# Batched causal attention feeding a maxout MLP: three TensorE score regions per group made two, with a tile of scores in the shared PSUM pool and early tokens copied first

## The chip, the cores and the metric

One core of a Trainium2 chip runs the whole kernel. The time is device microseconds of one launch; eight runs of the kernel before were taken. Tokens, heads and weights are all handled by that core, so the engines in question are its own: TensorE (PE), VectorE (DVE), ScalarE (ACT), GpSimd (POOL) and the queue that issues transfers (SP).

## The reference

Block-causal attention over 8 batches, 8 heads, 576 positions and head size 64, and behind it, on the same tokens, a maxout MLP:

```python
B, H, S, D = q.shape                      # 8, 8, 576, 64
scores = scale * np.matmul(q, k.transpose(0, 1, 3, 2))
mask = (pos[:, None] // 64) >= (pos[None, :] // 64)     # causal by blocks of 64
attn = exp(scores - max) / sum            # softmax over the allowed keys
x = (attn @ v).transpose(0, 2, 1, 3).reshape(B * S, H * D)   # 4608 tokens x 512
out = np.maximum(x @ w1, x @ w2) @ w_out  # 512 -> 1024 -> 512, float32
```

## The kernel before, in words

**Work units.** Heads are taken in pairs (`p`, 32 in all: 4 a batch), pairs in groups of two (`g`, 16 in all: 2 a batch). The two heads of a pair lie on partitions 0 to 63 and 64 to 127 and are multiplied as two 64-row tiles of the PE array side by side; everything with a contraction of 128 (the MLP, and attention times v) uses the whole array. A pair goes through: load and cast of q and k (`load_qk`, `cast`), 18 transposes of 64x64 for q and 18 for k of a whole group (`transposes`, L303) with a copy out of PSUM by DVE and ACT (`copy_out`, L310), scores (`scores`, L321, and `corner_scores`, L339), exp by ACT into `aT` (`exp`, L345, L401), zeroing of masked corners by POOL (`mask`, L350), attention times v in two groups of matmuls of 65 columns (`av`, L429: query tiles 0 and 1 with 6 matmuls, 2 to 4 with 24), a division by DVE (L435, L436), and transposes of the result into `xT` (`x_out`, L451, L453), which DVE copies out (L456, L457). `xT` is what the MLP reads.

**The MLP** is cut into spans of tokens (256, 320, then 512 each). For a span, `h_unit` makes eight times two accumulations of four matmuls (L197), one for w1 and one for w2: DVE copies the first out of PSUM (L204) and takes the maximum with the second (L206). `y_unit` makes eight matmuls with w_out (L215), copied out by ACT (by DVE for the first two spans, L221), and sent off. `units` lists all of these in order, `steps` matmul by matmul, and `fill(n)` emits the next `n` of them (in units of a 512-column matmul) if their tokens are done. So MLP matmuls are placed by hand between attention work, and all engines execute the order as it is written (`manual_schedule`).

**PSUM** has two pools: `ps_s`, two buffers of two banks each, for scores; `ps_m`, four buffers of one bank, for everything else: transposes, attention times v, x_out, h, y.

**Stages.** A prologue written out by hand covers batch 0 (groups 0 and 1): the scores of the first 256 queries first (`burst_p`), then those of the rest (`burst_q1` to `burst_q3`), so that the first 256 tokens reach the MLP early; `warm_up(n)` puts in matmuls of zeros whose result nobody reads. Then the loop over g from 2 to 15. In it each group has three stretches in which the array is in two 64-row tiles, called regions here: x_out of the group before with score tiles 0 and 1 of pair a; transposes of q with tile 2 of a and tile 0 of b; transposes of k with tiles 1 and 2 of b. In the second and third the exps come before the copies of the transposes:

```python
        for p, tiles in ((a, lambda: (tile_2(a), tile_0(b))), (b, lambda: (tile_1(b), tile_2(b)))):
            fill(hi)
            if g > GPB:
                av_with(p - LAG, lo)
            else:
                fill(lo)
            copy_out = t_pair(p)
            region(*tiles())
            copy_out()
```

Between regions `fill` emits MLP matmuls; `av_with` puts `lo = n // 18` of them between the two groups of a pair's attention times v. After the loop come the last pairs and what is left of the MLP.

Of the kernel before, what the change touches and what calls it, by code (L numbers as in the profile page):

```python
# [8 lines left out]
FP32 = mybir.dt.float32  # L9
# [5 lines left out]
def kernel(  # L15
# [95 lines left out]
    def load_qk(g, queues, gated=False):  # L111
        b, u = divmod(g, GPB)
        for nm, src, queue in (("q", q, queues[0]), ("k", k, queues[1])):
            if queue is None:
                continue
            raws[nm, g] = t = raw.tile([P, 2, RPP * D], FP32, name=f"{nm}raw")
            if gated:
                nc.gpsimd.memset(t[:, 0, :1], 0.0)
            queue.dma_start(
                out=t[:],  # L120
                in_=src[b, 4 * u:4 * u + 4].rearrange(
                    "(s h) (p t) d -> (h p) s (t d)", h=2, t=RPP),
            )

    def cast(nm, g, parts):
        t = raws.pop((nm, g)).rearrange("p s (t d) -> p t s d", d=D)
        qk_n[nm, g] = n = qkn.tile([P, RPP, 2, D], BF16, name=f"{nm}n")
        for copy, j0, j1 in parts:
            copy(out=n[:, j0:j1], in_=t[:, j0:j1])  # L129
# [12 lines left out]
    def load_w(f0, fw, which=(0, 1)):  # L142
        for i in which:
            dst, src = ((w1_sb, w1r), (w2_sb, w2r))[i]
            nc.gpsimd.dma_start(out=dst[:, :, f0:f0 + fw], in_=src[:, :, f0:f0 + fw])
# [11 lines left out]
    nc.vector.memset(zeros[:], 0.0)  # L157
    nc.scalar.activation(out=warm[:], in_=warm[:], func=AF.Exp)
    load_qk(1, (SP, SP))
    load_qk(2, (SP, None))  # L160
    make_identity(nc, ident)
    for r in range(NV):
        nc.vector.memset(vv_r[r][:, :, :, D:D + 1], 1.0)
# [9 lines left out]
    load_w(0, 256, (0,))  # L173
    cast("k", 1, ((pool, 0, RPP),))
    load_w(0, 256, (1,))
    load_qk(2, (None, SP), gated=True)


    done_tokens = [0]
# [88 lines left out]

    plan()
    steps = [(u, need, cost) for u, need, cost, n in units for _ in range(n)]  # L270
    at = [0]


# [4 lines left out]
            n += 1  # L278
        return int(total)

    def fill(n):
        while n > 0 and at[0] < len(steps) and steps[at[0]][1] <= done_tokens[0]:
            u, _, cost = steps[at[0]]
            next(u)
            n -= cost
            at[0] += 1


    def warm_up(n):
        pw = ps_m.tile([P, SPAN], FP32, name="ps_w", tag="m")  # L290
        for _ in range(n):
            nc.tensor.matmul(pw[:], zeros[:, :P], zeros[:], start=True, stop=True)
# [4 lines left out]
    def transposes(nm, g, copies):  # L297
        n = qk_n.pop((nm, g))
        pts = [ps_m.tile([P, RPP, NP], BF16, name=f"ps_{nm}T", tag="m") for _ in range(2)]
        for j in range(RPP):  # L300
            for i in range(2):
                r = slice(i * NP, (i + 1) * NP)
                nc.tensor.transpose(  # L303
                    pts[i][:, j, :], n[r, j].rearrange("p s d -> p (s d)"), ident[r, r],
                )

        def copy_out(which=(0, 1)):
            for i in which:
                t = (qT_r if nm == "q" else kT_r)[(2 * g + i) % NT]
                copies[i](  # L310
                    out=t[:, :S].rearrange("q (p j) -> q p j", j=RPP),
                    in_=pts[i].rearrange("q j p -> q p j"),
                )
        return copy_out

# [11 lines left out]
    def pad_keys(p):  # L327
        nc.gpsimd.tensor_copy(
            out=kz_r[p % NT].rearrange("p (a c) -> p a c", c=BLK)[:, 0:3:2],
            in_=kT_r[p % NT][:, S - 3 * BLK:].rearrange("p (a c) -> p a c", c=BLK)[:, 0:3:2],  # L330
        )


    def corner_scores(p, ps, col):
# [25 lines left out]
    def burst_p(p):  # L360
        burst(p, ((0, 0, QCUT), (1, P, QCUT - P)), 0)

    def burst_q1(p):
        burst(p, ((0, QCUT, 320), (1, QCUT, 192)), 384)

    def burst_q2(p):
        burst(p, ((1, 448, P), (2, QCUT, 320), (4, 512, BLK)), 896)
# [4 lines left out]
    def masks_p(p, eng=None):  # L372
        for a in (0, 256):
            mask(p, a, eng)
# [34 lines left out]
    def region(*tiles):  # L409
        for out in tiles:  # L410
            out()

    def av(p, ts):
        b, hp = divmod(p, HP)
        vv = vv_r[b % NV]
        a = aT_r[p % NA]
        n = len(ts)
        h0 = hp // 2 * 4 + hp % 2
        if p % 2 == 0 and ts[0] == 0:
            xps[p // 2] = xpool.tile([P, NCH, 2, 2, D], BF16, name="xp")  # L420
        xp = xps[p // 2]
        po = ps_m.tile([P, n, 2, D + 1], FP32, name="ps_o", tag="m")
        n_mm = 2 * sum(t + 1 for t in ts)
        mm = 0
        for gi, t in enumerate(ts):
            for hh in range(2):
                for c in range(t + 1):
                    a0 = a_col(p, c, t)
                    nc.tensor.matmul(  # L429
                        po[:, gi, hh, :], a[:, hh, a0:a0 + P], vv[:, c, h0 + 2 * hh, :],  # L430
                        start=(mm == 0), stop=(mm == n_mm - 1),
                    )
                    mm += 1
        rec = small.tile([P, 3, 2, 1], FP32, name="rec")
        nc.vector.reciprocal(rec[:, :n, :, 0], po[:, :, :, D])  # L435
        nc.vector.tensor_mul(  # L436
            xp[:, ts[0]:ts[0] + n, :, p % 2], po[:, :, :, :D],
            rec[:, :n].to_broadcast([P, n, 2, D]),
        )

    def x_out(g, t0=0, t1=NCH):
        b, u = divmod(g, GPB)
        xp = xps[g]
        n = t1 - t0
        n_odd = min(t1, NCH - 1) - t0
        pe = ps_m.tile([P, 2, n, BLK], BF16, name="ps_xe", tag="m")
        po = ps_m.tile([P, 2, n_odd, BLK], BF16, name="ps_xo", tag="m")
        for s in range(2):
            for t in range(t0, t1):
                src = xp[:, t, s].rearrange("p a d -> p (a d)")  # L450
                nc.tensor.transpose(pe[:, s, t - t0, :], src[:BLK], ident[:BLK, :BLK])  # L451
                if t < NCH - 1:
                    nc.tensor.transpose(po[:, s, t - t0, :], src[BLK:], ident[BLK:, BLK:])  # L453
        dst = xT[:, 2 * u:2 * u + 2, b * S + t0 * P:b * S + t1 * P].rearrange(
            "p s (t h w) -> p s t h w", h=2, w=BLK)
        nc.vector.tensor_copy(out=dst[:, :, :, 0], in_=pe[:])  # L456
        nc.vector.tensor_copy(out=dst[:, :, :n_odd, 1], in_=po[:])  # L457
        if u == GPB - 1:
            done_tokens[0] = min(b * S + t1 * P, (b + 1) * S)

# [37 lines left out]
        return lambda: [f() for f in outs]  # L498


    warm_up(16)
    cq = transposes("q", 0, (dve, act))
    ck = transposes("k", 0, (act, dve))
    cq((0,))
    ck((0,))
    cq((1,))
    ck((1,))
    cast("q", 1, ((dve, 0, RPP),))
    burst_p(0)
    masks_p(0)  # L510
    burst_p(1)
    warm_up(2)
    masks_p(1)
    for c in range(2, NCH):
        load_v(0, c)
    load_w(256, 256)
    cq = transposes("q", 1, (dve, dve))
    burst_q1(0)
    ck = transposes("k", 1, (dve, dve))
    for i in range(2):  # L520
        cq((i,))
        ck((i,))
    load_w(512, 512)
    warm_up(3)
    burst_p(2)
    av(0, [0, 1])
    burst_q3(0)
    warm_up(2)
    burst_p(3)
    masks_p(2, nc.vector)  # L530
    av(1, [0, 1])
    masks_p(3, nc.vector)
    burst_q2(0)
    av(2, [0, 1])
    warm_up(2)
    burst_q1(1)
    av(3, [0, 1])
    x_out(0, 0, 2)
    warm_up(2)
    cast("q", 2, ((pool, 0, RPP),))  # L540
    masks_q(0)
    cast("k", 2, ((pool, 0, RPP),))
    burst_q2(1)
    x_out(1, 0, 2)
    warm_up(2)
    burst_q3(1)
    masks_q(1)
    for c in range(3):
# [35 lines left out]
    def av_with(p, n):  # L584
        av(p, [0, 1])
        fill(n)
        av(p, [2, 3, 4])

    for g in range(GPB, NG):
        a, b = 2 * g, 2 * g + 1  # L590
        if x_due:
            x_out(x_due.pop())
        n = fill_of(g)
        region(tile_0(a), tile_1(a))
        if g == GPB:
            av(3, [2, 3, 4])
            fill(5)
            x_out(1, 2, NCH)
            n = fill_of(g)
        lo, hi = n // 18, n * 2 // 9  # L600
        for p, tiles in ((a, lambda: (tile_2(a), tile_0(b))), (b, lambda: (tile_1(b), tile_2(b)))):
            fill(hi)
            if g > GPB:
                av_with(p - LAG, lo)
            else:
                fill(lo)
            copy_out = t_pair(p)
            region(*tiles())
            copy_out()
            if p % 2 and g + 1 < NG:  # L610
                pad_keys(p + 1)
                pad_keys(p + 2)
            pool_work(p)
        if g > GPB:
            x_due.append(g - 1)
        fill(n - 2 * (lo + hi))
    for p in range(NPAIR - LAG, NPAIR):
        if x_due:
            x_out(x_due.pop())
# [40 lines left out]
```

The softmax here doesn't subtract the row's maximum and nothing guards it: scores larger than these inputs give would overflow.

## Time and profile before

| what | value |
|---|---|
| median of 8 runs (lowest, highest) | 287.0 us (286.38, 287.44) |
| the profiled execution's own time, and its span | 286.55 us, 284.7 us |
| granted TensorE clock | 1.00 |
| PE busy | 271.9 us, 96% of the span |
| DVE, ACT, POOL busy | 186.5, 140.8, 108.6 us |
| chain that ended last | PE 81%, issue 2%, ACT 2%, DVE 1% |

The span runs from the first to the last instruction of the program; 1.85 us of the execution lie around it. Busy time of PE is counted from modelled ends: a matmul of 512 columns has a row of 379 ns, while the next one starts 216 ns after it, so a busy PE isn't a PE without losses. How much is lost is read from start times.

### The profile page before, as it was taken

The numbers are of one execution on the slowest core, as the hardware profiler recorded it, in microseconds if no ns is written. First come the engines' busy times: TensorE is split into PE (matmuls) and PEld (weight loads), VectorE is DVE, ScalarE is ACT, GpSimd is POOL, SyncE is SP. The second block draws the span as 40 slices with busy tenths as digits, with TensorE's granted clock in tenths as the row PEclk, the third lists the DMA queues.
The fourth block names the chain that finished last, engine by engine and source line by source line (L and its number), as shares of the span: only waits on it lengthen the run. The fifth ranks groups of instructions, "written<-read, shape, count | busy, mean of one in ns | idle before, by whom it ended". The sixth has DMA issues, their size and how long they took to land.

```text
span 284.7 us, 7763 instructions
## 1 busy us (share of the span) xinstructions
PE 271.9 (96%) x3207; PEld 152.1 (53%) x3253; DVE 186.5 (65%) x386; ACT 140.8 (49%) x194; POOL 108.6 (38%) x271
## 2 busy tenths in 40 slices
PE   8799999899999999999999999999999999999995
PEld 2356666655555555555555464645555554444543
DVE  5867878768887576766666676667565765455430
ACT  3696567667566555573837556466454000110112
POOL 2996546764753634255243715462111000000000
PEclk9999999999999999999999999999999999999999
DMA  7999999949924893569363985176210112011114
GB/s 261 261 213 229 178 245 259 244 97 228 208 22 161 115 200 55 199 76 237 51 204 56 205 103 158 53 97 52 50 39 37 39 39 74 37 72 39 63 50 147
DMA packets 55939, 36.67 MB, mean 129 GB/s; under 512 B 38752, under 2 KB 43232, under 8 KB 55904
## 3 DMA queue, kind: packets, MB, share of 16 engines
q0 software_dynamic: 41728, 7.87, 34.7%
q1 hardware_dynamic: 13760, 27.66, 28.4%
q10 hardware_dynamic: 416, 0.66, 0.7%
q8 instruction: 25, 0.41, 0.6%
q14 instruction: 10, 0.08, 0.1%
HBM read 34.60 MB, written 9.44 MB: 155 GB/s over the span
## 4 chain that ended last, share of the span: by engine, by line
PE 81%; issue 2%; ACT 2%; DVE 1%; ACTq 0%
PE ps_h L197 39%; PE ps_y L215 21%; PE ps_o L429 9%; PE ps_s L321 6%; PE ps_qT L303 2%; PE ps_kT L303 2%; PE ps_xe L451 2%; ACT aT L345 1%; DVE g L206 1%; PE ps_y L231 1%; PE ps_s L339 1%; ACT qT L310 0%; ACT aT L401 0%; ACT kT L310 0%; PE ps_xo L453 0%
## 5 line engine op out<-in xcount | busy, mean ns | idle before, releaser
L197 PE MATMUL ps_h<-xT,w_sb 128*128 128x512 bf16 (+3 forms) x604 | 133.8, 357 | 4.0 <-issue 3.2
L345 ACT ACTIVATE aT<-ps_s 128x1024 bf16<-128x1024 f32 (+2 forms) x100 | 95.9, 993 | 62.2 <-PE ps_s L321 50.3
L197 PEld LDWEIGHTS <-w_sb 128*128 128x128 bf16 x640 | 57.4, 98 | 57.4 <-issue 8.4
L204 DVE CAST h<-ps_h 128x512 bf16<-128x512 f32 (+3 forms) x80 | 51.0, 638 | 29.6 <-PE ps_h L197 27.4
L215 PE MATMUL ps_y<-wo_sb,g 128*128 128x512 bf16 x273 | 65.5, 379 | 0.8 <-issue 0.5
L206 DVE TENSOR_TENSOR g<-h,ps_h 128x512 bf16<-128x512 bf16 (+3 forms) x80 | 50.7, 633 | 11.0 <-PE ps_h L197 8.9
L350 POOL MEMSET aT<- 64x128 bf16 x124 | 22.4, 199 | 92.5 <-ACT aT L345 91.5
L221 ACT COPY y<-ps_y 128x512 f32<-128x512 f32 x31 | 18.3, 591 | 71.4 <-PE ps_y L215 56.7
L429 PEld LDWEIGHTS <-aT 128*128 128x128 bf16 x960 | 37.0, 98 | 15.1 <-issue 3.9
L215 PEld LDWEIGHTS <-g 128*128 128x128 bf16 x280 | 27.0, 98 | 32.2 <-issue 1.1
L429 PE MATMUL ps_o<-vv,aT 128*128 128x65 bf16 x960 | 40.0, 194 | 0.5 <-DVE g L206 0.3
L133 POOL DMA_DIRECT2D vv<-in_v_dram x40 | 33.7, 847 | 0.5
L436 DVE TENSOR_TENSOR xp<-ps_o,rec 128x256 bf16<-128x256 f32 (+1 forms) x64 | 31.4, 491 | 2.2
L321 PE MATMUL ps_s<-qT,kT 64*128 64x64 bf16 (+6 forms) x344 | 31.8, 279 | 1.1 <-ACT kT L310 0.7
L435 DVE RECIPROCAL rec<-ps_o 128x4 f32<-128x4 f32 (+1 forms) x64 | 12.0, 187 | 23.7 <-PE ps_o L429 22.3
L187 POOL COPY g<-g 128x512 bf16<-128x512 bf16 x8 | 4.9, 612 | 38.5 <-DVE g L206 38.4
L129 POOL CAST kn<-kraw 128x1152 bf16<-128x1152 f32 x15 | 17.3, 1151 | 5.0 <-DMA kraw<-in_k_dram 5.0
L129 POOL CAST qn<-qraw 128x1152 bf16<-128x1152 f32 (+1 forms) x15 | 16.5, 1098 | 7.1 <-DMA qraw<-in_q_dram 7.0
L456 DVE COPY xT<-ps_xe 128x640 bf16<-128x640 bf16 (+2 forms) x18 | 8.2, 453 | 15.6 <-PE ps_xe L451 14.9
L321 PEld LDWEIGHTS <-kT 64*128 64x128 bf16 x344 | 13.6, 95 | 6.4 <-issue 2.8
L310 DVE COPY qT<-ps_qT 128x576 bf16<-128x576 bf16 x17 | 12.7, 749 | 1.1 <-PE ps_qT L303 1.1
L310 DVE COPY kT<-ps_kT 128x576 bf16<-128x576 bf16 x17 | 12.7, 750 | 0.2 <-PE ps_kT L303 0.2
(44 smaller groups left out, 142.4 us busy)
## 6 DMA issues: line engine op xcount, KB each, us to landing
qraw<-in_q_dram SPq DMA_DIRECT2D x16, 576.0 KB, 4.4
out_dram<-y SPq DMA_DIRECT2D x35, 256.0 KB, 2.7
kraw<-in_k_dram SPq DMA_DIRECT2D x15, 576.0 KB, 6.0
vv<-in_v_dram POOLq DMA_DIRECT2D x32, 128.0 KB, 5.6
w_sb<-in_moe_w_dram POOLq DMA_DIRECT2D x4, 256.0 KB, 6.5
w_sb<-in_moe_w_dram POOLq DMA_DIRECT2D x2, 512.0 KB, 11.3
wo_sb<-in_moe_w_out_dram POOLq DMA_DIRECT2D x2, 512.0 KB, 11.9
kraw<-in_k_dram ACTq DMA_DIRECT2D x1, 576.0 KB, 5.4
```

Of the source, the lines that this page charges most:

```text
L129: copy(out=n[:, j0:j1], in_=t[:, j0:j1])
L133: nc.gpsimd.dma_start(out=vv_r[b % NV][P - rows:, c, :, :D], in_=v[b, :, c * P:c * P + rows, :].rearrange("h p d -> p h d"),)
L197: nc.tensor.matmul(pt[:, :w], w_sb[:, c, f * P:(f + 1) * P], xT[:, c, t0:t0 + w], start=(c == 0), stop=(c == NDM - 1),)
L204: nc.vector.tensor_copy(out=h1[:, :w], in_=pt[:, :w])
L206: nc.vector.tensor_max(g[:, f, m:m + w], h1[:, :w], pt[:, :w])
L215: nc.tensor.matmul(py[:], g[:, f, s * P:(s + 1) * P], wo_sb[:, f, :], start=(f == 0), stop=(f == NFF - 1),)
L310: copies[i](out=t[:, :S].rearrange("q (p j) -> q p j", j=RPP), in_=pts[i].rearrange("q j p -> q p j"),)
L321: nc.tensor.matmul(ps[:, hh, col:col + w], kT[r, k0:k0 + P], qT[r, q0:q0 + w], start=True, stop=True,)
L345: nc.scalar.activation(out=aT_r[p % NA][:, :, a0:a0 + w], in_=ps[:, :, :w], func=AF.Exp, scale=scale,)
L350: (eng or nc.gpsimd).memset(aT_r[p % NA][BLK:, :, a0:a0 + BLK], 0.0)
L429: nc.tensor.matmul(po[:, gi, hh, :], a[:, hh, a0:a0 + P], vv[:, c, h0 + 2 * hh, :], start=(mm == 0), stop=(mm == n_mm - 1),)
L436: nc.vector.tensor_mul(xp[:, ts[0]:ts[0] + n, :, p % 2], po[:, :, :, :D], rec[:, :n].to_broadcast([P, n, 2, D]),)
```

## The change

1. **Loop, g from 2 on.** Two regions per group in place of three. Tile 0 gets its own function, `tile_0m`, which takes two buffers of `ps_m` (one bank for each head), computes head 1 first, and has its exps as two instructions of 512 columns. For pair a: x_out of the group before (its first copy by ACT), tile 1, tile 0, tile 2, transposes of q for the next group. For pair b: transposes of k, tile 1, tile 0, tile 2. The copies of the transposes are emitted ahead of the exps for b, and ahead of the last exp for a. `lo` is at least 3. `fill(..., True)` goes on to the end of an accumulation that has begun, so none is open across a region.
2. **Prologue.** The copies out of the transposes are split in two by token (261 of 576, then the rest); the first parts go first. In group 1 four of the eight parts go to ACT (before, all four copies were DVE's), and the two copies of the first x_out too. The bursts q1 to q3 of pairs 0 and 1 move behind the first 256 tokens' attention times v; with some MLP matmuls between them. 24 warm-up matmuls in place of 29.
3. **Loads.** q of group 2 is loaded together with its k, behind a POOL instruction, instead of at the very start. The weights' columns 256 to 511 are issued ahead of the last three loads of v, and columns 512 to 1023 in two blocks of 256 in place of one of 512, so POOL issues two transfers more.

```diff
     load_qk(1, (SP, SP))
-    load_qk(2, (SP, None))
...
-    load_qk(2, (None, SP), gated=True)
+    load_qk(2, (SP, SP), gated=True)
...
+    inside = [j % (NDM if n > NFF or n == 2 * NDM and u.__name__ == "h_unit" else NFF) > 0
+              for u, _, _, n in units for j in range(n)]
...
-    def fill(n):
-        while n > 0 and at[0] < len(steps) and steps[at[0]][1] <= done_tokens[0]:
+    def fill(n, whole=False):
+        while at[0] < len(steps) and steps[at[0]][1] <= done_tokens[0]:
+            if n <= 0 and not (whole and inside[at[0]]):
+                break
...
+    def tile_0m(p):
+        us = [ps_m.tile([P, 512], FP32, name="ps_s0", tag="m") for _ in range(2)]
+        for hh in (1, 0):
+            r = slice(hh * D, (hh + 1) * D)
+            nc.tensor.matmul(
+                us[hh][:], kT_r[p % NT][r, :P], qT_r[p % NT][r, :512], start=True, stop=True)
+
+        def out():
+            for hh in range(2):
+                nc.scalar.activation(
+                    out=aT_r[p % NA][:, hh, :512], in_=us[hh][:], func=AF.Exp, scale=scale)
+            mask(p, 0)
+        return out
...
-    cq((0,))
-    ck((0,))
-    cq((1,))
-    ck((1,))
+    cq((0,), LOW)
+    ck((0,), LOW)
+    ck((1,), LOW)
+    cq((1,), LOW)
+    cq((0,), HIGH)
     cast("q", 1, ((dve, 0, RPP),))
     burst_p(0)
     masks_p(0)
+    cq((1,), HIGH)
+    ck((0,), HIGH)
     burst_p(1)
+    ck((1,), HIGH)
...
+    cq = transposes("q", 1, (dve, act))
+    ck = transposes("k", 1, (dve, dve))
+    cq((0,), LOW)
+    cq((1,), LOW)
+    ck((0,), LOW)
+    ck((1,), LOW)
+    cq((0,), HIGH, act)
+    cq((1,), HIGH, dve)
+    load_w(512, 256)
+    load_w(768, 256)
+    warm_up(2)
+    burst_p(2)
+    ck((0,), HIGH, act)
+    av(0, [0, 1])
...
+    burst_p(3)
+    av(1, [0, 1])
+    ck((1,), HIGH, act)
...
+    av(2, [0, 1])
+    x_out(0, 0, 2, (act, act))
+    warm_up(1)
+    av(3, [0, 1])
     burst_q1(0)
+    warm_up(1)
+    x_out(1, 0, 2, (dve, dve))
+    burst_q2(0)
...
     for g in range(GPB, NG):
         a, b = 2 * g, 2 * g + 1
-        if x_due:
-            x_out(x_due.pop())
         n = fill_of(g)
-        region(tile_0(a), tile_1(a))
...
+        fill(0, True)
+        for p in (a, b):
+            if p == a and x_due:
+                x_out(x_due.pop(), copies=(act, dve))
+                n = fill_of(g)
+            if p == a:
+                out1 = tile_1(a)
+                out0 = tile_0m(a)
+                out2 = tile_2(a)
+                copy_out = t_pair(a) if g > GPB else (lambda: None)
+                out0()
+                out1()
+                copy_out()
+                out2()
+            else:
+                copy_out = t_pair(b)
+                out1 = tile_1(b)
+                out0 = tile_0m(b)
+                out2 = tile_2(b)
+                copy_out()
+                out1()
+                out0()
+                out2()
...
+            lo = max(3, n // 18)
+            hi = max(0, n // 2 - lo)
             if g > GPB:
+                fill(hi * 3 // 5)
                 av_with(p - LAG, lo)
+                fill(hi - hi * 3 // 5, True)
             else:
-                fill(lo)
...
+                fill(lo + hi, True)
```

More of the change, by code (lines that the diff above doesn't have):

```diff
@@ L305, in transposes, with copy_out @@
                 )
-        def copy_out(which=(0, 1)):
+        def copy_out(which=(0, 1), part=(0, NP), copy=None):
+            p0, p1 = part
             for i in which:
                 t = (qT_r if nm == "q" else kT_r)[(2 * g + i) % NT]
-                copies[i](
-                    out=t[:, :S].rearrange("q (p j) -> q p j", j=RPP),
-                    in_=pts[i].rearrange("q j p -> q p j"),
+                (copy or copies[i])(
+                    out=t[:, p0 * RPP:p1 * RPP].rearrange("q (p j) -> q p j", j=RPP),
+                    in_=pts[i][:, :, p0:p1].rearrange("q j p -> q p j"),
                 )
@@ L439, in av, with x_out @@
         )
-    def x_out(g, t0=0, t1=NCH):
+    def x_out(g, t0=0, t1=NCH, copies=(dve, dve)):
         b, u = divmod(g, GPB)
@@ L455, in x_out @@
             "p s (t h w) -> p s t h w", h=2, w=BLK)
-        nc.vector.tensor_copy(out=dst[:, :, :, 0], in_=pe[:])
-        nc.vector.tensor_copy(out=dst[:, :, :n_odd, 1], in_=po[:])
+        copies[0](out=dst[:, :, :, 0], in_=pe[:])
+        copies[1](out=dst[:, :, :n_odd, 1], in_=po[:])
         if u == GPB - 1:
@@ L498, in t_pair @@
         return lambda: [f() for f in outs]
+    LOW = (0, -(-QCUT // RPP))
+    HIGH = (LOW[1], NP)
     warm_up(16)
@@ L510 @@
     masks_p(0)
+    cq((1,), HIGH)
+    ck((0,), HIGH)
     burst_p(1)
+    ck((1,), HIGH)
     warm_up(2)
     masks_p(1)
+    load_w(256, 256)
     for c in range(2, NCH):
         load_v(0, c)
-    load_w(256, 256)
-    cq = transposes("q", 1, (dve, dve))
-    burst_q1(0)
[L519 to L526, printed above, removed]
-    burst_q3(0)
[L528 to L540, printed above, removed]
+    cq = transposes("q", 1, (dve, act))
[12 more added lines that the diff above has]
+    av(0, [0, 1])
+    masks_p(2, nc.vector)
+    burst_p(3)
+    av(1, [0, 1])
+    ck((1,), HIGH, act)
+    masks_p(3, nc.vector)
+    warm_up(1)
[3 more added lines that the diff above has]
+    av(3, [0, 1])
+    burst_q1(0)
+    warm_up(1)
+    x_out(1, 0, 2, (dve, dve))
+    burst_q2(0)
+    warm_up(1)
+    cast("q", 2, ((pool, 0, RPP),))
+    fill(2)
+    burst_q3(0)
     masks_q(0)
     cast("k", 2, ((pool, 0, RPP),))
+    burst_q1(1)
+    fill(1)
     burst_q2(1)
-    x_out(1, 0, 2)
-    warm_up(2)
+    fill(1)
     burst_q3(1)
@@ L590 @@
         a, b = 2 * g, 2 * g + 1
-        if x_due:
-            x_out(x_due.pop())
         n = fill_of(g)
-        region(tile_0(a), tile_1(a))
[L595 to L602, printed above, removed]
+        fill(0, True)
[21 more added lines that the diff above has]
+                out2()
+                if g + 1 < NG:
+                    pad_keys(p + 1)
+                    pad_keys(p + 2)
+            pool_work(p)
+            if g == GPB and p == a:
+                av(3, [2, 3, 4])
+                fill(5)
+                x_out(1, 2, NCH)
+                t_pair(a)()
+                n = fill_of(g)
+            lo = max(3, n // 18)
+            hi = max(0, n // 2 - lo)
             if g > GPB:
+                fill(hi * 3 // 5)
                 av_with(p - LAG, lo)
+                fill(hi - hi * 3 // 5, True)
             else:
-                fill(lo)
[L607 to L613, printed above, removed]
+                fill(lo + hi, True)
         if g > GPB:
             x_due.append(g - 1)
-        fill(n - 2 * (lo + hi))
     for p in range(NPAIR - LAG, NPAIR):
```

## The prediction

> **What bounds the kernel now.** I read the page's busy times and its chain first:
>
> ```profile
> PE 271.9 (96%) x3207; PEld 152.1 (53%) x3253; DVE 186.5 (65%) x386; ACT 140.8 (49%) x194; POOL 108.6 (38%) x271
> ...
> PE 81%; issue 2%; ACT 2%; DVE 1%; ACTq 0%
> ```
>
> PE sets the end. Its matmuls are the same before and after, warm-ups apart, so the question is how long it stands still between them. That is read from start times in the timeline; here PE around one region (start, duration, then what it was and how many):
>
> ```profile
> 114.00 0.59 PE L197 MATMUL ps_h<-xT,w_sb 128*128 128x512 bf16 x2
> 114.53 0.20 PE L451 MATMUL ps_xe<-ident,xp 64*128 64x64 bf16 x1
> ...
> 114.80 0.19 PE L451 MATMUL ps_xe<-ident,xp 64*128 64x64 bf16 x1
> 114.83 0.59 PE L321 MATMUL ps_s<-qT,kT 64*128 64x512 bf16 x5
> 115.36 0.61 PE L197 MATMUL ps_h<-xT,w_sb 128*128 128x512 bf16 x2
> ```
>
> Two 512-column matmuls from 114.00 at 216 ns each have streamed by 114.43. The next of that kind starts at 115.36: 0.93 us. Work in between: 18 transposes, 0.27 us, and three score pairs, two heads side by side, (512 + 64 + 448) / 2.4 = 0.43 us. So a region costs 0.23 to 0.26 us above its work: 0.10 going in (114.43 to 114.53), 0.13 coming out, the rest within. Regions repeated every 15.2 us in the loop show 0.23 to 0.30 each; I use 0.26.
>
> One group in that loop takes 15.2 us: 48 MLP matmuls x 0.216 = 10.4, 60 of attention times v x 0.029 = 1.7, three sets of transposes 0.8, scores of two pairs 1.3, together 14.2. Of the 1.0 us lost, three regions explain 0.78 and a wait in the attention times v 0.14 (the matmul stream stops that long at 92.0, 107.2, 122.4, ...).
>
> What a wait on DVE costs PE is seen in the chain of waits near 66 us (start, duration):
>
> ```profile
> 64.95 1.26 PE ps_h L197 x5
> 66.20 0.02 issue
> 66.23 0.70 DVE g L206
> 66.93 0.04 issue
> 66.97 0.89 PE ps_o L429 x24
> ```
>
> The last of five h matmuls starts at 65.83 and has streamed by 66.05. DVE's maximum with it begins at 66.23, ends at 66.93, and the matmul that needed its bank starts at 66.97: **0.92 us from the end of the stream to the next use of that bank**.
>
> The prologue is another stage (busy time and count of PE, PEld, DVE, ACT, POOL; clock; DMA share; GB/s):
>
> ```profile
> 8.00:21.00 13.00, 10.82 (x186) 6.15 (x186) 10.35 (x26) 10.92 (x15) 12.31 (x23) 1.00 1.69 227
> 92.00:205.00 113.00, 110.25 (x1386) 61.40 (x1407) 76.20 (x149) 64.67 (x90) 49.68 (x125) 1.00 0.63 120
> ```
>
> From 8 to 21 us ACT is busy 10.92 of 13 us and PE waits for exps; in the loop (second line) ACT has 43% of its time free.
>
> [...]
>
> **The change part by part**, against the profiled execution's own 286.55 us (span 284.7 and 1.85 around it).
>
> (1) Fewer regions. Before, the loop has four in g = 2 and three in each of 13 more groups, 43; the order of the changed kernel has three and then two, 29. 14 x 0.26 = **-3.6 us**. Sure within 0.5[...].
>
> (2) Tile 0 in the shared pool: the new wait. All four ps_m buffers are in use in a region, two of transposes (or x_out) and two of tile 0. The order of the changed program gives head 0 of tile 0 the bank of the very last h (or y) before the region, so its matmul waits for DVE's L206. That bank is free 0.92 us after the stream's end. PE arrives earlier: 0.10 in, 0.27 transposes, tile 1 (64 + 448) / 2.4 = 0.21, so at 0.58. It stands for **0.34 us**, and tile 2, the transposes of q and the next h stand behind it. Head 1, done first, needs the cast of the half before (L204), which has ended by then. 24 regions (g = 4 to 15): 24 x 0.34 = +8.2. In g = 2 and 3 the spans are 256 and 320 wide, DVE's maximum takes 0.42 to 0.49 in place of 0.69, about 0.1 each: +0.4. **+8.6 us**; bounds 6 (arrival 0.1 later) and 10.5. Before, scores had their own two buffers and no region waited like this.
>
> (3) Way out of pair a's region. The next h takes the bank of tile 0's head 0, so it waits for the first half exp. ACT: x_out copy first (0.55 to 1.2 us after the stream's end; 0.63 for 576 columns), the exp when head 0 is there (1.14 + 0.18), 0.59 for 512 columns (the row of the y copy, the nearest), so the bank comes at 1.95; PE, with (2), would be ready at 1.8. 13 x 0.15 = **+2.0 us**, bounds 0 and 3.9. Pair b's next h takes a transposes' bank, free by 1.2, PE at 1.5: nothing. The copies ahead of the exps thus do work there; their cover is PE's own score matmuls, without them up to 0.2 a group.
>
> (4) At least three MLP matmuls between the AV groups: removes two waits of 0.33 (66.4, 78.4) and nine of 0.14. **-1.9 us**; bounds -1.9 and 0, since the third matmul alone is worth 0.22 of cover.
>
> (5) Prologue. Added on ACT: four half copies of group 1, 2 x 0.64 plus two splits; two more splits in group 0; two copies of x_out. A split costs an instruction's fixed part, from the rows 1023 ns at 1024 columns and 488 at 384: 0.17 us. Together 1.28 + 4 x 0.17 + 2 x 0.38 = 2.7 us, on an engine that had 2.1 us free there. In return DVE is relieved of 2 us and the first h comes about 0.4 us sooner (before: 18.0 us). But q1 to q3 of pairs 0 and 1, 6 us of exps, now stand largely behind it, with little MLP between. Followed by hand, the first long AV group starts about 2 us later (20.2 before), with 8 to 10 more h matmuls of 0.11 done: **+1.2 us**, bounds -0.5 and +2.5.
>
> (6) Loads. q of group 2 moves from SP's start to behind POOL's memset at 11 us; it lands in 4 to 7 us, POOL casts it (1.15), PE wants it near 21: hidden; without cover it would be 1 to 2 us, inside (5)'s bound. On POOL the w issues (0.75 each) pass the last three v loads, which start 1.5 us later and land near 22, when PE reaches them: 0.3 at worst. Two more w issues queue ahead of that cast. Both are in (5)'s bounds. `fill(..., True)` only moves MLP matmuls; the ends of accumulations cost nothing. ACT's split exps and the x_out copy in the loop, about 0.4 us a pair, lie in its free 43%.
>
> Sum: -3.6 + 8.6 + 2.0 - 1.9 + 1.2 = +6.3; 286.55 + 6.3 = 292.9. The median of the runs before is 0.45 above the profiled one, so a median of about **293.0 us**.
>
> **The rivals.** A: regions are saved and nothing waits (faster). It decides if PE comes to head 0 of tile 0 later than 0.92 us after the last h, for instance because the transposes themselves wait 0.35 for their banks or casts, or DVE's copy is nearer than I read. Then (2) and (3) fall: -3.6 - 1.9 + 1.2, about 282.5. For it: before, some regions of the first 60 us lost 0.4 to 0.8 to such waits, and if the new order frees them 1 to 1.5 us more is gained. Against: the order puts the last maximum ahead of tile 0 in nearly all regions, and the 0.92 is measured. B: ACT decides. Its chain in the prologue costs the full 2.5, and the ways out of a wait up to 0.3, so 286.55 + 6.3 + 1.3 + 1.9, about 296 to 297. Against: 43% free in the loop. C: half of (2) is covered by waits that exist anyway; +2, about 289. D: the parts cancel, 287.
>
> **How the numbers follow.** What a measurement of this kernel can tell from no change is about 0.2%, 0.57 us. The main case 0.62 (289.5 to 296), B 0.10, C 0.12, D 0.04, A 0.12. Slower 0.84, same 0.04, faster 0.12. The main case's own range is 289.5 to 296; to 8 in 10 it takes in C and part of D and B: 287.0 to 296.5.
>
> **What would show it.** In the profile after: waits of ps_s0 (the second of its two matmuls) on DVE L205 or its like, 0.3 us a region, some 20 to 26 of them; [...]a group of the loop at 15.7 us in place of 15.2; no stop of 0.14 or 0.33 in the AV groups; the first long AV group near 22 us. I am wrong if a group takes 15.0 us or less, or if ps_s0 waits for nothing.

## The result, and the profile after

The median went from 287.0 us (31 runs) to **298.8 us** (11 runs, 296.2 to 301.7); the ratio is 1.0403, with a 95% interval of 1.0383 to 1.0423. The direction was forecast, the size was not: +11.8 us in place of +6, outside the range. The profiled execution after took 298.2 us (span 296.4), against 286.55: +11.65. The mean granted clock was 0.982 to 0.994 in all 11 runs after; of the 72 runs of before that were timed beside the experiments below, 3 had a mean under 0.995.

The page after, busy times and chain:

```profile
PE 279.8 (94%) x3207; PEld 152.1 (51%) x3248; DVE 180.5 (61%) x374; ACT 150.0 (51%) x242; POOL 109.1 (37%) x274
...
PE 85%; ACT 4%; issue 3%; DMA 3%; POOL 2%; DVE 2%; ACTq 0%; POOLq 0%; DVEq 0%
```

PE still sets the end, with as many matmul rows in the trace, but DMA and POOL are on the chain now. PE's busy time grew by 7.9 us. That is partly a modelled end that stretches over a stop (0.72 us in place of 0.38 in tile 0's row below), and partly a slower clock, which stands in one digit of the page's row (tenths of full speed, 40 slices):

```profile
PEclk9997999999999999999999999999999999999999
```

Before, every digit was a 9. To find where the time went I took, in both traces, the moment at which PE had done equal amounts of its work, warm-ups left out:

| work done, us | before at | after at | behind by |
|---|---|---|---|
| 2 | 13.85 | 13.01 | -0.8 |
| 5 | 19.48 | 20.61 | +1.1 |
| 7 | 22.37 | 26.72 | **+4.4** |
| 35 | 56.53 | 61.80 | +5.3 |
| 50 | 73.02 | 79.62 | **+6.6** |
| 180 | 213.34 | 225.11 | **+11.8** |
| 246 | 281.43 | 293.20 | +11.8 |

The two kernels emit this work in different orders, so a row is good to about half a microsecond, the first one to less.

So there are three stretches: the prologue (+4.4), groups 2 to 5 (+2.2; group 6 begins near 50 us of work), groups 6 on (+5.2). The last is the loop that was forecast; the first is where I was furthest off. Some expectations below call the second stretch groups 2 to 4; by its regions it reaches through group 5.

**The loop.** A group takes 15.75 us (its regions of pair a begin at 92.69, 108.44, 124.19), forecast 15.7, before 15.20. PE in pair b's region, the answer to the region shown of before:

```profile
100.83 0.44 PE L306 MATMUL ps_kT<-ident,kn 64*128 64x64 bf16 x18
101.11 0.38 PE L325 MATMUL ps_s<-qT,kT 64*128 64x64 bf16 x4
101.33 0.72 PE L342 MATMUL ps_s<-qT,kT 64*128 64x512 bf16 x2
...
102.23 1.04 PE L196 MATMUL ps_h<-xT,w_sb 128*128 128x512 bf16 x4
```

The merged row of tile 0 (L342) is 0.72 us long, one such matmul 0.38: so the second head started at about 101.67, 0.34 behind the first. What it waited for is in DVE's timeline, the maximum of the last h, over at 101.63:

```profile
100.94 0.69 DVE L205 TENSOR_TENSOR g<-h,ps_h 128x512 bf16<-128x512 bf16 x1 [0.17 <-PE ps_h L196]
```

Measured by start times as before, each b region loses 0.59 us above its work, 0.26 + 0.33. Each a region loses 0.88: the same, and 0.28 on the way out, which the list of waits (total, times, longest) names in this stretch:

```profile
PE ps_h L196 <- ACT aT L347: 1.9, 8, 0.2
```

The chain of waits shows that way out (start, duration): tile 0's two heads, the half exp, the next h.

```profile
93.37 0.16 PE ps_s L342
...
93.54 0.39 PE ps_s L342
...
94.01 0.60 ACT aT L347
94.61 0.04 issue
94.65 0.38 PE ps_h L196
```

**The prologue.** POOL before, from its v loads to the cast of q2 (`qn`):

```profile
11.80 2.44 POOL L133 DMA_DIRECT2D vv<-in_v_dram  x3
14.21 3.01 POOL L145 DMA_DIRECT2D w_sb<-in_moe_w_dram  x4
17.27 1.14 POOL L129 CAST qn<-qraw 128x1152 bf16<-128x1152 f32 x1
```

and after:

```profile
13.22 2.46 POOL L133 DMA_DIRECT2D vv<-in_v_dram  x3
15.63 1.54 POOL L145 DMA_DIRECT2D w_sb<-in_moe_w_dram  x2
19.01 0.75 POOL L145 DMA_DIRECT2D w_sb<-in_moe_w_dram  x1 [1.84 <-DMA w_sb<-in_moe_w_dram]
21.10 0.74 POOL L145 DMA_DIRECT2D w_sb<-in_moe_w_dram  x1 [1.34 <-DVE h L203]
21.89 1.14 POOL L129 CAST qn<-qraw 128x1152 bf16<-128x1152 f32 x1
```

The two added block issues stand 3.2 us in the queue. The first waits for a w block issued at 10.24, eight of POOL's issues earlier, which landed 8.49 us later, at 18.73. The second is put down to an h copy that nothing here depends on. But the block eight issues before it, issued at 11.75, landed at 20.82, and both issues begin 0.28 us after such a landing; in e2 and e9 below the same stop is put down to a landing w block. q2's own data had landed at 17.60; behind the two issues its cast comes 4.6 us later than before, and PE stands still for it:

```profile
20.61 0.39 PE L325 MATMUL ps_s<-qT,kT 64*128 64x320 bf16 x4
23.09 0.60 PE L306 MATMUL ps_qT<-ident,qn 64*128 64x64 bf16 x18 [2.08 <-POOL qn L129]
23.62 1.46 PE L196 MATMUL ps_h<-xT,w_sb 128*128 128x256 bf16 x6
25.02 0.60 PE L325 MATMUL ps_s<-qT,kT 64*128 64x128 bf16 x6
25.55 1.36 PE L448 MATMUL ps_o<-vv,aT 128*128 128x65 bf16 x24
```

Then the granted clock falls (stretches; busy time and count of PE, PEld, DVE, ACT, POOL; clock, DMA share, GB/s). The clock of a stretch is a mean: the 0.80 is 1.00 up to 23.15 us and 0.50 from 23.25 on.

```profile
22.00:24.00 2.00, 0.91 (x20) 0.73 (x21) 0.28 (x1) 0.25 (x2) 1.88 (x4) 0.80 2.07 168
24.00:26.00 2.00, 2.00 (x21) 1.14 (x19) 0.90 (x2) 0.79 (x2) 1.94 (x5) 0.50 1.49 195
```

From q2's transposes to the first long AV group (the 24 matmuls of attention times v) it took 2.46 us, before 1.45. That AV group starts at 25.55 us; 22 was forecast, 20.2 it was before. The clock was 0.50 up to 26.4 us and 1.00 again from 26.7 on. The fall came behind a standstill of 2.1 us; that the one brought about the other was an estimate of mine, which e4 below tests.

### The profile page after: what moved, and what is told of

Same layout as the page of the kernel before. It is cut to its first block, busy times and chain, and to the rows that moved or that the text cites. A ratio compares the mean times of both kernels' runs of the same rounds, so it can differ in the third digit from the quotient of the medians.

```text
span 296.4 us, 7823 instructions
## 1 busy us (share of the span) xinstructions
PE 279.8 (94%) x3207; PEld 152.1 (51%) x3248; DVE 180.5 (61%) x374; ACT 150.0 (51%) x242; POOL 109.1 (37%) x274
## 4 chain that ended last, share of the span: by engine, by line
PE 85%; ACT 4%; issue 3%; DMA 3%; POOL 2%; DVE 2%; ACTq 0%; POOLq 0%; DVEq 0%
PE ps_h L196 41%; PE ps_y L214 20%; PE ps_o L448 10%; PE ps_s L325 4%; PE ps_s L342 4%; DMA w_sb<-in_moe_w_dram 3%; ACT aT L347 3%; PE ps_w L295 2%; PE ps_kT L306 2%; PE ps_xe L470 2%; POOL qn L129 1%; PE ps_qT L306 1%; PE ps_y L230 1%; ACT aT L364 1%; DVE xp L455 1%
## 5 line engine op out<-in xcount | busy, mean ns | idle before, releaser
L196 PE MATMUL ps_h<-xT,w_sb 128*128 128x512 bf16 (+3 forms) x615 | 137.6, 359 | 4.2 <-ACT aT L347 2.1
L364 ACT ACTIVATE aT<-ps_s 128x1024 bf16<-128x1024 f32 (+2 forms) x72 | 71.5, 1000 | 8.7 <-PE ps_s L325 8.4
L214 PE MATMUL ps_y<-wo_sb,g 128*128 128x512 bf16 x265 | 69.6, 379 | 1.1 <-ACT aT L347 0.2
L205 DVE TENSOR_TENSOR g<-h,ps_h 128x512 bf16<-128x512 bf16 (+3 forms) x80 | 50.7, 633 | 14.1 <-PE ps_h L196 11.8
L214 PEld LDWEIGHTS <-g 128*128 128x128 bf16 x280 | 24.7, 98 | 23.6 <-issue 0.6
L325 PE MATMUL ps_s<-qT,kT 64*128 64x128 bf16 (+5 forms) x288 | 31.8, 263 | 0.7 <-ACT kT L314 0.5
L347 ACT ACTIVATE aT<-ps_s 128x512 bf16<-128x512 f32 x56 | 30.5, 603 | 3.2 <-PE ps_s L342 2.0
L314 ACT COPY kT<-ps_kT 128x576 bf16<-128x576 bf16 (+2 forms) x18 | 10.6, 589 | 24.5 <-PE ps_kT L306 24.5
L314 DVE COPY qT<-ps_qT 128x576 bf16<-128x576 bf16 (+2 forms) x18 | 12.4, 690 | 13.0 <-PE ps_qT L306 12.8
L342 PE MATMUL ps_s<-qT,kT 64*128 64x512 bf16 x56 | 19.3, 375 | 0.2
L475 ACT COPY xT<-ps_xe 128x640 bf16<-128x640 bf16 (+1 forms) x13 | 8.7, 667 | 20.1 <-PE ps_xe L470 20.0
```

Of the source, the lines that this page charges most:

```text
L196: nc.tensor.matmul(pt[:, :w], w_sb[:, c, f * P:(f + 1) * P], xT[:, c, t0:t0 + w], start=(c == 0), stop=(c == NDM - 1),)
L205: nc.vector.tensor_max(g[:, f, m:m + w], h1[:, :w], pt[:, :w])
L214: nc.tensor.matmul(py[:], g[:, f, s * P:(s + 1) * P], wo_sb[:, f, :], start=(f == 0), stop=(f == NFF - 1),)
L325: nc.tensor.matmul(ps[:, hh, col:col + w], kT[r, k0:k0 + P], qT[r, q0:q0 + w], start=True, stop=True,)
L342: nc.tensor.matmul(us[hh][:], kT_r[p % NT][r, :P], qT_r[p % NT][r, :512], start=True, stop=True)
L347: nc.scalar.activation(out=aT_r[p % NA][:, hh, :512], in_=us[hh][:], func=AF.Exp, scale=scale)
```

## The experiments

Times are medians; before had 286.8 to 287.3 beside them. "Behind by" means as in the table above.

**e1 and e2: one half of the change each.** e1 has the loads and prologue of before and the new loop; e2 the reverse.

> The loads and the prologue of the kernel before, with the loop of the changed kernel. Theory (of the 11.8 us lost, 4.4 are lost up to 27 us, where the prologue is, and the rest in the loop): 298.8 - 4.4 = 294.4 us, a group of the loop at 15.75 us, the first long AV group near 20.2 us, and clock 1.00 throughout. Rival (the late prologue starts a chain of late casts that the loop then repeats, so the loop alone is cheap): 290 us or less, with PE's waits for the cast qn at 45 and 68 us gone.

> The loads and the prologue of the changed kernel, with the loop of the kernel before. Theory: 287.0 + 4.4 = 291.4 us, a group at 15.2 us, the first long AV group near 25.5 us. Rival (what the prologue loses is given back later, because MLP matmuls that it pushes back find other gaps): 288 to 289 us.

Measured: e1 293.7 us, ratio 1.0233 (1.0194 to 1.0272); e2 291.3 us, 1.0142 (1.0105 to 1.0180). The halves bring +6.4 and +4.1, 10.5 of 11.8; the rest isn't assigned. Both theories hold: in e1 the first long AV group starts at 19.9 us, and groups 2 to 5 lose 2 us, the rest of the loop 5, as in the full change; in e2 that group starts at 24.3 us (25.5 was expected), and behind 26 us hardly anything is lost (0.3 us) and nothing given back. So the loss of the loop isn't inherited from the prologue.

**e3: two POOL issues fewer.**

```diff
-    load_w(512, 256)
-    load_w(768, 256)
+    load_w(512, 512)
```

> The changed kernel with the last two blocks of w1 and w2 loaded as one pair of 512 columns, as before: two DMA issues fewer on POOL ahead of the cast of q2. Theory (POOL stands still at the two extra issues until older transfers have landed, and the cast, PE's transposes of q2 and the clock follow): POOL casts q2 about 3 us sooner, the first long AV group near 22.5 us, clock 1.00 there, time 298.8 - 3 = 295.8 us. Rival (the added half copies and x_out copies on ACT set the prologue's end): no gain over 0.5 us, 298.3 to 299.3.

Measured: 298.6 us, no gain. The rival has the number, but the trace doesn't show its reason. PE in e3:

```profile
20.73 0.44 PE L306 MATMUL ps_qT<-ident,qn 64*128 64x64 bf16 x18
...
22.20 0.23 PE L448 MATMUL ps_o<-vv,aT 128*128 128x65 bf16 x2
24.25 0.37 PE L448 MATMUL ps_o<-vv,aT 128*128 128x65 bf16 x7 [1.81 <-DMA vv<-in_v_dram]
25.69 1.00 PE L448 MATMUL ps_o<-vv,aT 128*128 128x65 bf16 x15 [1.07 <-DMA vv<-in_v_dram]
```

The cast (17.8 us) and q2's transposes came sooner, and the first long AV group began at 22.2, as the theory had it. Then it stood for v, issued between 13.5 and 15.9 us. One late transfer was exchanged for another. The theory's clock of 1.00 did not come either: it was 0.74 from 24 to 26 us and 0.50 from 26 to 28, behind these waits.

**e4: the clock.** Ten warm-up matmuls ahead of q2's transposes, to fill the standstill.

```diff
+    warm_up(10)
     transposes("q", 2, (dve, act))()
```

> The changed kernel with ten warm-up matmuls (2.2 us) ahead of the transposes of q2, in the time in which PE stands still. Theory (the standstill also lowers the granted clock to 0.50, which costs 1.0 us up to the first long AV group and 0.3 in it): clock 0.95 to 1.00 from 22 to 28 us, time 298.8 - 1.3 = 297.5 us. Rival (the lower clock costs nothing, since PE waits for POOL and ACT there anyhow): 298.8 us; if the warm-ups last longer than the wait, up to 299.2.

Measured: 297.4 us, against the changed kernel's 298.8; its profile has a clock of 1.00 from 20 to 28 us, q2's transposes at 23.13 (23.09 without the warm-ups), and the AV group at 24.58 in place of 25.55. So **1.0 us** of the prologue's loss is the clock, by the traces; the medians (-1.4) agree, though their spread (1.0332 to 1.0423) would not show it alone. Four of the six runs had a mean clock of 1.000 and took 297.2 to 297.6 us; the other two had 0.994 and took 299.0 and 300.6, so the warm-ups do not always prevent the dip.

**e5: POOL's order of before**, v ahead of w and the w pair whole, q2 still gated.

```diff
-    load_w(256, 256)
     for c in range(2, NCH):
         load_v(0, c)
+    load_w(256, 256)
...
-    load_w(512, 256)
-    load_w(768, 256)
+    load_w(512, 512)
```

> The changed kernel with POOL's DMA issues in the order of the kernel before: the three v loads of batch 0 ahead of the w blocks, and the last two w blocks as one pair. With the pair alone the cast of q2 came early, but PE then waited 1.8 and 1.1 us for v loads that landed near 24 and 26 us. Theory (the two effects together, late v or late q2 cast, are what the prologue loses): PE waits for neither, the first long AV group starts near 22 us, clock 1.00, and 298.8 - 3.3 = 295.5 us. Rival (with both cured, the exps on ACT or the gated q2 load take their place): 297.5 us or more.

Measured: 297.3 us, next to the rival's number and far from the theory's. In its profile yet another transfer is late, the w block that the earlier MLP matmuls want:

```profile
21.29 0.61 PE L196 MATMUL ps_h<-xT,w_sb 128*128 128x256 bf16 x2 [2.93 <-DMA w_sb<-in_moe_w_dram]
```

and POOL waited 2.98 us for q2's own data; the clock was 0.50 from 22 to 26 us. With every order something lands late, which pointed at the amount to be moved in that stretch. From 8 to 10 us, before, then after (last number GB/s):

```profile
8.00:10.00 2.00, 1.04 (x13) 0.36 (x10) 2.00 (x3) 1.93 (x4) 1.59 (x3) 1.00 1.11 373
```

```profile
8.00:10.00 2.00, 0.94 (x9) 0.43 (x10) 2.00 (x5) 1.84 (x5) 1.39 (x2) 1.00 1.86 160
```

Gating q2 takes its 0.59 MB out of this stretch and puts them behind 11 us, beside w and v.

**e9, e10: q2 early again.** e9 is the changed kernel with q2's load alone put back; e10 has e5's order as well, so all loads as before.

```diff
+    load_qk(2, (SP, None))
...
-    load_qk(2, (SP, SP), gated=True)
+    load_qk(2, (None, SP), gated=True)
```

> The changed kernel with q of group 2 loaded at SP's start again, as before; nothing else. Theory (from 8 to 10 us the DMA engines moved 373 GB/s before and 160 after, since q2's 0.59 MB now fall into the crowded stretch behind 11 us; each mended POOL order only made another transfer late): the w blocks and v land sooner, POOL's two extra issues stand less, PE's stop ahead of q2's transposes falls from 2.1 to under 0.5 us, clock 1.00, 298.8 - 3.0 = 295.8 us. Rival (POOL's order of issues decides, not when q2 is loaded): 298 us or more.

> The changed kernel with all loads as before: q2 at SP's start, v ahead of w, the last w pair whole. What stays of the new prologue is the order of copies and bursts. Theory (the loads make the prologue's loss, the added work on ACT little): the first long AV group near 21 us and 294 to 295 us, as with the old prologue under the new loop (293.7), plus up to 1. Rival (the added copies on ACT cost the 1.2 to 2.5 us of the forecast as well): 295.5 to 296.5 us.

Measured: e9 295.8 us (1.0295, 1.0253 to 1.0336), e10 295.6 us (1.0292, 1.0245 to 1.0339). At 7 us of work e9 is behind by 2.0 and e10 by 1.1, in place of 4.4. e9's theory holds, with PE's wait at the transposes down to 0.32 us; its clock fell to 0.50 earlier instead, from 16 to 18 us, which the theory did not have. In e10's profile the clock is 1.00 and the AV group starts at 22.7. Its rival has the number: against e1, which has the same loop and loads, e10 is 1.9 us longer. Three of e10's six runs had a lower mean clock; the three at 1.000 took 294.8 to 295.3 us, 1.5 more than e1. The two intervals overlap. So the order of copies and bursts, without the loads, costs some 1.5 to 1.9 us, inside the forecast's -0.5 to +2.5.

**e11 and e13: the gate alone, in the kernel before.** The inverse of e9's edit, run twice; e11's profiled execution took 705 us, so only e13's trace is read.

> The kernel before with one part of the change alone: q of group 2 gated behind POOL's memset at 11 us. Theory (the same 0.59 MB in the crowded stretch): cast of q2 waits for its data until 19.5 to 20 us, q2's transposes about 2 us late, maybe a lower clock behind it: 287.0 + 2 to 3 = 289 to 290 us. Rival (the load is hidden, as the forecast had it): 287.0 us, within 0.6.

> The kernel before with q of group 2 gated behind POOL's memset, once more, since the profiled execution of the first such run was disturbed and shows no usable trace. Theory: from 8 to 10 us the DMA engines move about 160 GB/s in place of 373; POOL's cast of q2 starts at 20 us or later in place of 17.3, waiting for the data; q2's transposes follow 2 us or more late; 290 to 291.5 us. Rival (the time went elsewhere, to w or v): the cast within 1 us of before.

Measured: 291.2 us (1.0127, 1.0075 to 1.0179) and 290.8 us (1.0100, 1.0049 to 1.0151): by the ratios **+3 to 4 us for one line**. e13's POOL and its DMA rate:

```profile
18.74 1.14 POOL L129 CAST qn<-qraw 128x1152 bf16<-128x1152 f32 x1 [1.34 <-PE ps_s L320]
```

```profile
8.00:10.00 2.00, 1.22 (x10) 0.43 (x10) 2.00 (x3) 2.00 (x4) 1.47 (x3) 1.00 1.80 176
```

The cast is 1.5 us late, less than expected. The idle time is put down to a PE matmul, but the q2 load, the cast's own input, landed at 18.59. The w block issued next to it, at 10.46, took 10.3 us to land, against 5.3 before. PE waits 1.4 us for the cast, 0.5 for a w block and 0.4 for v, and from 22 to 28 us the clock is 0.50 to 0.54. So the lost transfer time spreads over q2, w and v.

How much the low clock takes can be seen from run to run. In e13 one run had a mean clock of 1.000 and took 288.3 us; the three at 0.987 took 290.6 to 291.1. In e11 two runs at 0.999 and 1.000 took 289.7 and 289.8 us; three at 0.988 to 0.994 took 290.8 to 292.5. So the moved load alone costs 1 to 3 us, and the low clock, in the runs that have it, 1 to 3 more. These are few runs, and the split is an estimate from them.

**e6, e7: tile 2 ahead of tile 0**, in pair b's regions (e6, shown), and in a's (e7, the same two lines).

```diff
-                out0 = tile_0m(b)
                 out2 = tile_2(b)
+                out0 = tile_0m(b)
```

> The changed kernel, in pair b's regions with tile 2's scores ahead of tile 0's. Theory (PE stands 0.34 us for the bank of the last h, which is free 0.92 us after the matmul stream's end; coming 0.24 us later, it waits 0.10): a b region loses 0.36 us above its work in place of 0.59, 12 regions x 0.24 = 2.9 us less, 295.9 us. Rival (the loss is not this wait but the half-bank exps or the copies of the transposes): no change, 298.3 to 299.3 us.

> The changed kernel with the same swap in pair a's regions. Theory (there the next h waits for the first half exp, and that for tile 0's head 0, whose bank is free at the same time in either order): PE waits less going in and more coming out, an a region stays at 0.88 us, time 298.8 us, or up to 1 us longer. Rival (both waits simply add up, and the first can be saved as in b): 298.8 - 2.9 = 295.9 us.

Measured: e6 298.3 us, e7 298.6 us. The medians are inside the spread of the runs (e6 ran from 296.6 to 300.5), so the traces have to tell. Tile 0 in a b region of e6:

```profile
102.10 0.48 PE L342 MATMUL ps_s<-qT,kT 64*128 64x512 bf16 x2
102.63 0.59 PE L196 MATMUL ps_h<-xT,w_sb 128*128 128x512 bf16 x2
```

The pair takes 0.48 us in place of 0.72, so head 0's stop fell from 0.33 to about 0.1: the bank of the last h it is. The region's loss fell less, from 0.59 to 0.45 (100.40 and each one behind it); about 0.1 came in between the last score and the next h, and why was not tried. It makes 1.7 us in 12 regions in place of 2.9. In e7 the a regions stay at 0.88, as its theory had it, and the wait on the way out grows:

```profile
PE ps_h L196 <- ACT aT L347: 2.3, 8, 0.3
```

The two waits of an a region hang on one chain: bank, head 0, half exp, next h.

**e8, e12: the three matmuls alone**, in the kernel before, everywhere (e8) or from group 5 on (e12).

```diff
-        lo, hi = n // 18, n * 2 // 9
+        lo, hi = max(3, n // 18), n * 2 // 9               # e8
+        lo, hi = max(3 if g > 4 else 0, n // 18), n * 2 // 9   # e12
```

> The kernel before with at least three MLP matmuls between a pair's two AV groups in place of n // 18 (which gave two or none), the one part alone. Theory (the third matmul takes away two stops of 0.33 us and nine of 0.14): 287.0 - 1.9 = 285.1 us. Rival (the matmul is missing elsewhere, ahead of the next region, and the stop turns up there): 287.0 us.

> The kernel before with at least three MLP matmuls between AV groups from g = 5 on only. Theory (in the run with it everywhere, the loop behind 65 us gained 1.7 us and groups 2 to 4 lost 2.5, where PE then waited for copies of transposes and for a w block): 287.0 - 1.7 = 285.3 us, faster than both kernels. Rival (the gain of the later groups is only the earlier groups' loss given back): 287.0 us.

Measured: e8 286.9 us, ratio 0.9985 (0.9969 to 1.0002); e12 286.0 us, 0.9983 (0.9961 to 1.0005). In e8 a group of the loop takes 15.0 us in place of 15.2, so the term has its size there; but by 65 us of work it is behind by about 2.5 us, its own waits ahead of 74 us being these:

```profile
PE ps_o L429 <- ACT qT L310: 1.2, 2, 0.8
PE ps_h L197 <- DMA w_sb<-in_moe_w_dram: 1.0, 1, 1.0
PE ps_xo L453 <- ACT kT L310: 0.6, 1, 0.6
```

It gives some 1.6 back and comes out even in the medians: the rival's number, though the stops are not where the rival put them. e12 still falls behind, by 0.7 us between 40 and 65 us of work, before it gains about 1.5. Its median is the lowest of all kernels here, 0.8 us under before, but the interval takes in 1: a version that beats both is not shown.

**e14: POOL's casts first**, in pair b's regions, for the waits of groups 2 to 5.

```diff
                 out2 = tile_2(b)
+                if g + 2 < NG:
+                    cast("q", g + 2, ((pool, 0, RPP),))
+                    cast("k", g + 2, ((pool, 0, RPP),))
                 copy_out()
```

(and the same casts taken out of `pool_work`)

> The changed kernel with POOL's casts of q and k of group g + 2 ahead of the masks, key pads and gated memsets of pair b's region instead of behind them. Theory (in groups 2 to 4 PE's transposes wait for these casts because POOL does them last): the regions at 43.6 and 67 us fall from 1.4 to about 0.9 us, the one at 49.6 from 0.73 to 0.6, together 1.2 us, 297.6 us. Rival (the raw q and k have not landed by then, so the masks now stand behind the casts): the waits move to PE's attention times v, 298.8 us or more.

Measured: 304.4 us, ratio 1.0588 (1.0554 to 1.0623): the rival, in a form that it had not named. POOL stood 4.4 us for k of group 4, with the key pads behind the cast, and a corner score waited for the pads:

```profile
PE ps_s L358 <- POOL kz L332: 5.1, 1, 5.1
```

The edit moved two casts, and it is k's data that came late. In the changed kernel PE waits for the cast of q at 45 us, and that one did not wait for data: the load of that q, issued at 39.29, took 3.9 us and had landed at 43.18. POOL did other work first:

```profile
43.94 0.34 POOL L369 MEMSET aT<- 64x128 bf16 x2 [0.72 <-ACT aT L364]
44.34 0.52 POOL L332 COPY kz<-kT 128x128 bf16<-128x128 bf16 x2
...
44.88 1.15 POOL L129 CAST qn<-qraw 128x1152 bf16<-128x1152 f32 x1
```

So for q the trace points to the order, as the theory had it, and e14 failed by the cast of k that it moved along. Moving q's cast alone was not tried. At 67 us, in group 5 (72 us in e14), the wait for the cast is gone, and the region fell from 1.39 to 1.15; a wait of 0.3 us for `xp` from DVE is still in it.

## Why the prediction failed, by its own steps

| stretch | forecast | trace |
|---|---|---|
| prologue, steps (5) and (6) | +1.2 | +4.4 |
| groups 2 to 5, out of (1) to (4) | about +0.8 | +2.2 |
| groups 6 on, the rest of (1) to (4) | +4.3 | +5.2 |
| sum | +6.3 | +11.8 |

The forecast for groups 2 to 5 is four regions fewer (-1.0), four stops of 0.1 and four of 0.34 (+1.8), three ways out (+0.4), one AV stop (-0.3).

Three figures that the prediction works with stand in the trace of before. Its 2.4 columns a nanosecond are 512 columns in 216 ns (2.37), rounded. The two heads do run side by side: six score matmuls, 2048 columns in all, start from 114.78 us on, and the next h starts at 115.36, 0.58 us later; one behind the other, at 216 ns for 512 columns, they would take 0.86. And the end of an accumulation shows no loss: from 95.78 to 98.80 us fourteen 512-column matmuls, six of h and eight of y, take 3.02 us, 216 ns each.

**Step (6) failed, and it is the largest miss.** It called q2's gated load hidden, 1 to 2 us without cover. It had looked at when q2 lands, and there it was right (6.5 us after its issue, forecast 4 to 7), and not at what the load moves aside: v was to land near 22 us and landed at 24.0 to 25.5. e11 and e13 price the gate alone at 3 to 4 us, and e9 gains 3.0 without it. Step (6) also placed PE's need near 21 us, while the trace of before has the transposes at 18.78. And it left the two added w issues "in (5)'s bounds" by their 0.75 us each; the 3.2 us that POOL stood at them was not in the sum, since an issue was taken to cost only its own time. The lower clock behind a standstill, 1.0 us in the trace after, was in no step.

**Step (5) was about right.** With the loads as before, the new order of copies and bursts costs 1.5 to 1.9 us (e10 against e1), forecast +1.2. Rival B's full 2.5 there is not reached. Its way out of 0.3 is close to the 0.28 found, though, and e10 does not separate ACT's added copies from the order of the bursts.

**Steps (1) and (2) hold.** Head 0's stop is 0.33 us, forecast 0.34, behind the operation that was named, and tile 2 stood behind it (its first matmul starts at 101.69). Without that stop the 0.59 us of a region of pair b are the 0.26 of before. But the sign that I gave was wrong: the list of waits shows no wait of `ps_s0`, since the stop lies under head 1's modelled duration of 0.38 us; it shows only in start times. It had its full size from group 4 on, as step (2) took it, but for one region at 67.6 us, where PE came late for another reason.

**Step (3) was mis-sized:** 0.28 in place of 0.15. The half exp is as long as it was put (0.60 us), but it begins 1.41 us after the stream's end and not 1.32, so that the next h starts at 2.05 in place of 1.95; PE would be ready near 1.77, forecast 1.8. It stayed inside the bounds; over the ten groups from 6 on it makes 1.3 us, more than the 0.9 that this stretch came out above its forecast.

**Step (4) held in the loop and not in the sum.** No AV stop is left in the trace after; the same edit alone (e8) makes a group 0.2 us shorter and loses that in the groups ahead.

**Groups 2 to 5** were summed as if they were the steady loop. From 36 to 73 us PE's transposes wait 1.3 us for casts, about what this stretch lost above its forecast, and in no step:

```profile
PE ps_qT L306 <- POOL qn L129: 1.3, 2, 1.0
```

By the traces both come from POOL's order of work: at 45 us the cast began 1.7 us after its data had landed, and at 67 us e14 took the wait away. That the whole 1.3 us could be had without loss elsewhere is not shown.

The sum at the end of the prediction has a slip as well: 286.55 + 6.3 + 0.45 makes 293.3, not 293.0. Nothing hangs on it.

## What to carry to other kernels

Before a load is delayed, look at what the transfers did in the stretch that it leaves and in the one that it enters: here a load taken out of a stretch at 373 GB/s came back as a late weight, a late value or a late cast, whichever was wanted first. Price an added transfer by the queue it stands in, not by its issue time: two issues of 0.75 us each stood 3.2 us here. And cost a stage that is not periodic from its own trace: rates read in the loop held there to a tenth of a microsecond and said little of the first 70 us.

## What the hardware showed unexpectedly

A standstill of PE of 2.1 us was followed by a clock of 0.50 for some 3 us (23.25 to 26.4 us after); in e13 it was 0.50 to 0.54 for 6 us, behind waits of 1.4, 0.5 and 0.4. In e9 the clock fell to 0.50 from 16 to 18 us with no PE wait over 0.6 us ahead of it, only a stretch in which PE was busy 1.4 and 1.6 of 2 us; in the kernel before PE was busy 1.0 and 1.1 of 2 us from 8 to 12 us, with waits of up to 0.7, and the clock stayed at 1.00. So in these traces the length of a stop does not tell by itself whether the clock falls. Ten matmuls of zeros in the gap kept it at 1.00 in e4's profile and in four of its six runs.
